# Turning the normalised attention outputs on VectorE instead of through DRAM by DMA

## The chip, the core and the metric

The kernel runs on one core of a Trainium2 chip. The core has TensorE (PE, matrix products into PSUM), VectorE (DVE), ScalarE (ACT), GpSimd (POOL) and SyncE (SP, which here only issues DMAs). They run side by side and wait for each other through semaphores. The metric is the device time of one execution in microseconds, lower is better; the time before is the median of three runs.

## The reference

Two pairs of layers work on x of 2048 rows by 512 columns, in bf16: a spectral filter, then an attention with 32 query heads of 16 columns and a single key and value head.

```python
x = x + _A_ref(_layernorm(x, axis=-1), A_w_r, A_w_i)      # A: irfft2(rfft2(x) * W)
x = x + _B_ref(_layernorm(x, axis=-1), B_wq, B_wk, B_wv, B_wo)
x = x + _A_ref(_layernorm(x, axis=-1), A_w_r, A_w_i)
x = x + _B_ref(_layernorm(x, axis=-1), B_wq, B_wk, B_wv, B_wo)
...
scores = jnp.einsum("bhqd,bkd->bhqk", q, k) * (Dh ** -0.5)   # in _B_ref
p = _softmax(scores, axis=-1)
o = jnp.einsum("bhqk,bkd->bhqd", p, v)
return (lambda x, *d: x.transpose(*d))(o, 0, 2, 1, 3).reshape(B, S, H * Dh) @ wo
```

## The kernel before, in words

**Stages.** Each pair is one `Layer`. Its front normalises rows, transposes them and runs the first Fourier matmuls; its middle and back (`add_middle`, `add_back`) finish the filter and make keys, values and the first query tiles; then its attention (`Attn`) runs. Fronts of the second layer for finished rows run inside the first layer's attention.

**Attention.** It is cut into 32 blocks: four query blocks of 512 rows (`qb`), four groups of eight heads (`g`), and two halves of a group (`par`), four heads each. A block has 16 key blocks of 128 and so 64 score tiles ("units") of 128 keys by 512 queries. The scores of four heads run side by side in four 32-row strips of TensorE. The exponential of a unit is taken in one of two ways. ScalarE takes an exact exp over two units at a time from a double PSUM bank `sa` (`exp`, L1346). VectorE takes an approximation from a single bank: one `tensor_scalar` makes a 16-bit integer whose bits are a bf16 number (`p1`, L1353), and two more phases, integer additions mostly on GpSimd (`phase`, L1357, or on VectorE, L1359), refine it. So an exact unit costs TensorE one value matmul (`pv`, L1363) and an approximated one three. Each value matmul also sums the weights, in a 17th column.

**Closing a block.** When the values of a block are summed, VectorE transposes the accumulator in 32x32 blocks into `raw` (`evac`, L1370). After the second half of a pair it takes reciprocals of the sums (`recip`, L1375) and multiplies (`mul`, L1381) into `on`, bf16, 128x512, with two buffers. `on` has queries in its partitions, and the output projection needs head columns there: it must be turned once more in blocks. In this kernel fifteen of the sixteen pairs of a layer go through DRAM: `norm_dma` issues four DMAs that write 32 partitions each into `onw` (L1401) and one transposing DMA that reads it back into `OT` (L1402), all from SP's queue. The last pair of a layer is turned by VectorE (`norm`, L1390).

**After four pairs of a query block.** `close_rows` adds the output projection (`proj`, L1406: four row tiles of four matmuls), the addition to x on VectorE (`close_x`, L1276; at the end of the first layer the addition is a fifth matmul instead, with statistics L1050 read from PSUM), and in the first layer the front of the next layer. For the last query block the projection of the first three groups is one task and that of the fourth another.

**What sets the order.** There is no loop order by hand. A planner (`Plan`) walks through modelled time, keeps modelled clocks of the four engines, and emits each engine's instructions in the order that comes out; on the chip the engines follow this order and semaphores. Units are dealt to ScalarE or VectorE by `deadline`: whoever would run dry first gets the next scores. All other work is a `Task` with an engine, a modelled duration, dependencies, a priority and perhaps a `lazy` time during which it only takes free moments. A `Mark` is an event without an instruction. For the turn by DMA the planner sets a mark at the end of the multiplication plus `OUT_TURN`, 25 us, before which nothing that reads the turned tile is placed. Query tiles of later groups (`add_qt`, L1325 on TensorE and L1285 for the copy) are tasks as well, asked for three blocks ahead. Where TensorE would be idle too long, `fill` emits matmuls on zeros (`dummy`, L1032 and L1036).

Of the kernel before, what the change touches and what calls it, by code (L numbers as in the profile page):

```python
# [10 lines left out]
P = 128  # L11
BF = mybir.dt.bfloat16
# [102 lines left out]
class Plan:  # L115
# [30 lines left out]
    PATIENT = 1000.0  # L146
    URGE = 150.0
    TURN = 7000.0
    OUT_TURN = 25000.0
    EARLY_SD = 0  # L150
    STARVED = 12000.0

# [442 lines left out]
class Attn:  # L595
# [74 lines left out]
    def done(self, b, slot, end):  # L670
        p, em = self.plan, self.em
        qb, g, par = self.blocks[b]
        self.left.discard(b)
        m = Mark("PE", end, slot)
        ev = p.add("DVE", 630.0, [m], lambda k: em.evac(self, b, slot), give=(m,), prio=-3)
        self.evac[b] = self.evac_last = ev
        if par == 0:
            return
        tail = 0.0 if b >= len(self.blocks) - 2 else 5000.0
        rc = p.add("DVE", 260.0, [ev, self.evac[b - 1]], lambda k: em.recip(self, b), lazy=tail)  # L680
        mu = p.add("DVE", 600.0, [rc], lambda k: em.mul(self, b), lazy=tail, port=True)
        if b < len(self.blocks) - 2:
            no = Mark("DMA", None)

            def turned(k):
                em.norm_dma(self, b)
                no.end = k.end + p.OUT_TURN

            mu.then = turned
        else:  # L690
            no = p.add("DVE", 626.0, [mu], lambda k: em.norm(self, b), lazy=tail)
        self.evac[b] = no
        if g == 3:
            self.layer.close_rows(qb, [self.evac[8 * qb + 2 * i + 1] for i in range(4)])
# [252 lines left out]
class Emit:  # L947
# [441 lines left out]
            at.OT[qb] = self.t4([4, 512])  # L1389
        self.nc.vector.transpose(out=at.OT[qb][:, g, :], in_=on.rearrange("p a h d -> p (a h d)"))  # L1390

    def norm_dma(self, at, b):

        qb, g, par = at.blocks[b]
        on = at.raw.pop((qb, g))
        if g == 0:
            at.OT[qb] = self.t4([4, 512])
        way = self.way.tile([512, P], BF, name="onw", tag="onw")
        rows = way.rearrange("(a q) (h c) -> h q a c", q=32, c=32)
        for h in range(4):  # L1400
            self.nc.sync.dma_start(out=rows[h], in_=on[32 * h:32 * h + 32].rearrange("p a h d -> p a (h d)"))  # L1401
        self.nc.sync.dma_start_transpose(out=at.OT[qb][:, g:g + 1, :], in_=way)  # L1402

    def proj(self, at, t, r, slot, g0, g1):
        for g in range(g0, min(g1, 4)):
            self.nc.tensor.matmul(self.ps(slot), lhsT=at.OT[t][:, g, r * P:(r + 1) * P], rhs=self.WO[:, g, :],  # L1406
                                  start=(g == 0), stop=(g == g1 - 1), skip_group_check=True)
# [89 lines left out]
```

## Time and profile before

| what | us |
|---|---|
| median of 3 runs | 1332.8 (1332.57 to 1332.93) |
| the profiled execution: its time, and its span | 1332.57, 1330.8 |
| first layer, attention: first to last approximated tile starts | 111.4 to 671.1 |
| second layer, attention: the same | 768.9 to 1318.3 |
| the 120 copies to DRAM: issue to landing, median | 1.9 |
| the 30 transposing DMAs, on their queue | 1.12 to 1.24 each |

In the profile, times count from the start of the span. "Busy" counts from the start of an operation to its end, and since the end of one overlaps the start of the next, starts of neighbours on a full engine stand closer together than the operations last. L numbers are lines of the kernel before. A line of the view in order of time has start, duration, engine, source line, operation, output and inputs with shapes, and in brackets the idle time before it and what ended it.

### The profile page before, as it was taken

To read this page: it belongs to the slowest core of one execution; us is meant where nothing else is said; L and a number is where in the kernel's file an instruction comes from. 1 tells how busy PE (TensorE), PEld (TensorE's weight loads), DVE (VectorE), ACT (ScalarE), POOL (GpSimd) and SP (SyncE) were. 2 spreads that over 40 slices of the span, in tenths; PEclk is the share of its full clock that TensorE was granted. 3 is DMA by queue.
4 is the path that set the end of the run, shared out by engine and by line. 5 is a ranking of instruction groups with operands and counts; after the bars stand their busy time and mean duration, and the time that the engine had idled before them with its cause. 6 is when DMAs were issued, how large, how long until landed. Compare 5 with 4: busy or idle time off the path is not lost. (4 is left out here: it accounts for less than half of the span.)

```text
span 1330.8 us, 31765 instructions
## 1 busy us (share of the span) xinstructions
PE 1291.0 (97%) x12968; PEld 438.2 (33%) x13032; DVE 1273.3 (96%) x2280; ACT 1226.4 (92%) x1396; POOL 842.0 (63%) x826
## 2 busy tenths in 40 slices
PE   9999999999999999999999999999999999999998
PEld 4643222222222223332256422223222322322232
DVE  6998999999999999999979999999999999999998
ACT  6478999999999999999954899999999999999996
POOL 0004787857777667766720067887677867786785
PEclk9999999999999999999999999999999999999999
DMA  9100000010000100010051000000100010000001
GB/s 294 41 1 1 10 9 10 10 41 10 5 7 12 39 9 10 9 41 10 9 166 41 1 1 9 10 10 9 25 10 10 10 25 6 9 14 22 5 9 25
DMA packets 108722, 33.05 MB, mean 25 GB/s; under 512 B 88352, under 2 KB 107296, under 8 KB 108576
## 3 DMA queue, kind: packets, MB, share of 16 engines
q1 hardware_dynamic: 108288, 30.46, 10.0%
q8 instruction: 102, 1.67, 0.5%
q10 hardware_dynamic: 288, 0.56, 0.1%
q14 instruction: 44, 0.36, 0.1%
HBM read 17.89 MB, written 7.60 MB: 19 GB/s over the span
## 5 line engine op out<-in xcount | busy, mean ns | idle before, releaser
L1341 PEld LDWEIGHTS <-KA 32*128 32x128 bf16 x2048 | 87.6, 91 | 234.1 <-issue 222.9
L1341 PEld LDWEIGHTS <-KB 32*128 32x128 bf16 x2048 | 85.2, 91 | 229.7 <-issue 224.1
L1363 PEld LDWEIGHTS <-vs_116 128*32 128x32 bf16 x2474 | 98.3, 94 | 97.2 <-issue 90.8
L1363 PEld LDWEIGHTS <-vs_117 128*32 128x32 bf16 x1622 | 97.7, 94 | 62.8 <-issue 60.6
L1363 PEld LDWEIGHTS <-vs_118 128*32 128x32 bf16 x1622 | 71.0, 93 | 75.6 <-issue 72.8
L1363 PEld LDWEIGHTS <-vs_119 128*32 128x32 bf16 x1622 | 72.0, 94 | 65.5 <-issue 57.5
L1357 POOL INT64_ADD w_1388<-w_1387 x1 | 1.0, 1039 | 110.5 <-DVE w_1387 L1353 110.5
L1357 POOL INT64_ADD w_11001<-w_11000 x1 | 1.0, 1037 | 98.3 <-PE b_69 L1341 98.3
L1050 DVE BATCH_NORM_STATS2 st<-x_sb 128x6 f32<-128x512 bf16 x52 | 35.4, 681 | 4.1 <-DMA x_sb<-in_A_x_dram 3.6
L1346 ACT ACTIVATE e_8_92<-sa_65 128x1024 bf16<-128x1024 f32 x32 | 35.5, 1110 | 2.4 <-PE sa_64 L1341 1.6
L1346 ACT ACTIVATE e_6_90<-sa_64 128x1024 bf16<-128x1024 f32 x33 | 36.5, 1106 | 0.0
L1346 ACT ACTIVATE e_13_97<-sa_65 128x1024 bf16<-128x1024 f32 x31 | 34.7, 1118 | 1.6 <-PE sa_64 L1341 1.6
L1346 ACT ACTIVATE e_1_85<-sa_64 128x1024 bf16<-128x1024 f32 x32 | 35.4, 1107 | 0.0
L1346 ACT ACTIVATE e_5_89<-sa_65 128x1024 bf16<-128x1024 f32 x30 | 33.5, 1118 | 1.6 <-PE sa_64 L1341 1.6
L1346 ACT ACTIVATE e_12_96<-sa_65 128x1024 bf16<-128x1024 f32 x31 | 34.1, 1100 | 0.9 <-PE b_69 L1341 0.8
L1346 ACT ACTIVATE e_19_103<-sa_65 128x1024 bf16<-128x1024 f32 x31 | 34.7, 1121 | 0.1
L1346 ACT ACTIVATE e_10_94<-sa_65 128x1024 bf16<-128x1024 f32 x30 | 33.2, 1106 | 1.7 <-PE sa_64 L1341 1.6
L1346 ACT ACTIVATE e_18_102<-sa_64 128x1024 bf16<-128x1024 f32 x31 | 34.6, 1115 | 0.1
L1346 ACT ACTIVATE e_2_86<-sa_65 128x1024 bf16<-128x1024 f32 x30 | 33.5, 1116 | 1.3 <-PE sa_64 L1341 1.0
L1346 ACT ACTIVATE e_9_93<-sa_64 128x1024 bf16<-128x1024 f32 x31 | 34.6, 1115 | 0.1
L1346 ACT ACTIVATE e_7_91<-sa_65 128x1024 bf16<-128x1024 f32 x31 | 34.4, 1110 | 0.1
L1346 ACT ACTIVATE e_15_99<-sa_64 128x1024 bf16<-128x1024 f32 x31 | 34.3, 1107 | 0.1
(4100 smaller groups left out, 6438.4 us busy)
## 6 DMA issues: line engine op xcount, KB each, us to landing
it<-const_IT SPq DMA_DIRECT2D x8, 640.0 KB, 6.1
onw<-on SPq DMA_DIRECT2D x120, 32.0 KB, 1.9
x_sb<-in_A_x_dram SPq DMA_DIRECT2D x4, 512.0 KB, 6.8
out_dram<-x_sb SPq DMA_DIRECT2D x16, 128.0 KB, 1.9
way<-x_sb SPq DMA_DIRECT2D x6, 256.0 KB, 2.4
tab_PH<-const_PH ACTq DMA_DIRECT2D x1, 512.0 KB, 4.9
w_131<-const_FT SPq DMA_DIRECT2D x1, 512.0 KB, 8.8
w_136<-const_FT SPq DMA_DIRECT2D x1, 512.0 KB, 8.4
```

The lines of the kernel that those rows point to most:

```text
L1050: self.nc.vector.bn_stats(st, self.ps(slot) if slot else self.x[:, x[1], x[0], :])
L1341: self.nc.tensor.matmul(o, lhsT=KX[rs, kc * P:(kc + 1) * P], rhs=at.QT[qb][rs, g, :], start=True, stop=True, skip_group_check=True)
L1346: self.wrote("ACT", e, self.nc.scalar.activation(out=e, in_=self.ps(slot), func=ACT.Exp, scale=SCALE))
L1357: self.nc.gpsimd.int64_add(t[p][:, 0:n].bitcast(U64), t[0][:, 0:n].bitcast(U64), DELTA[p] * FOUR)
L1363: self.nc.tensor.matmul(self.ps(slot)[32 * h:32 * h + 32, :], lhsT=V[:, kc, :], rhs=rhs, start=first, stop=last, skip_group_check=True)
```

## The change

All outputs are turned on VectorE by `norm`, as the last pair of each layer already was. The branch that called `norm_dma`, the function itself and the constant `OUT_TURN` go. The turn is now a task with a modelled 626 ns and the same `lazy` time as the multiplication (5 us, and none for the last pair); the tasks that read the turned tile wait for its end instead of for the mark 25 us after the multiplication.

```diff
-    OUT_TURN = 25000.0
...
         mu = p.add("DVE", 600.0, [rc], lambda k: em.mul(self, b), lazy=tail, port=True)
-        if b < len(self.blocks) - 2:
-            no = Mark("DMA", None)
-
-            def turned(k):
-                em.norm_dma(self, b)
-                no.end = k.end + p.OUT_TURN
-
-            mu.then = turned
-        else:
-            no = p.add("DVE", 626.0, [mu], lambda k: em.norm(self, b), lazy=tail)
+        no = p.add("DVE", 626.0, [mu], lambda k: em.norm(self, b), lazy=tail)
         self.evac[b] = no
...
-    def norm_dma(self, at, b):
-
-        qb, g, par = at.blocks[b]
-        on = at.raw.pop((qb, g))
-        if g == 0:
-            at.OT[qb] = self.t4([4, 512])
-        way = self.way.tile([512, P], BF, name="onw", tag="onw")
-        rows = way.rearrange("(a q) (h c) -> h q a c", q=32, c=32)
-        for h in range(4):
-            self.nc.sync.dma_start(out=rows[h], in_=on[32 * h:32 * h + 32].rearrange("p a h d -> p a (h d)"))
-        self.nc.sync.dma_start_transpose(out=at.OT[qb][:, g:g + 1, :], in_=way)
```

Since the planner deals all work anew, the change of one task's engine moves the order on every engine from the first closed pair on.

## The prediction

> **What bounds the kernel now.** I read the busy totals first, then the forty slices, then the busy time of each engine in stretches, and last the order of time on VectorE and ScalarE where a stretch was not full.
>
> ```profile
> span 1330.8 us, 31765 instructions
> PE 1291.0 (97%) x12968; PEld 438.2 (33%) x13032; DVE 1273.3 (96%) x2280; ACT 1226.4 (92%) x1396; POOL 842.0 (63%) x826
> ...
> DVE  6998999999999999999979999999999999999998
> ACT  6478999999999999999954899999999999999996
> ```
>
> The totals name three engines as candidates. The slices say where: VectorE and ScalarE are both full in the two attention stages (about 111 to 672 and 769 to 1319 us) and are short of work only in the spectral stages before each. TensorE's 97% is made of modelled ends, so I ask who waits for whom instead. The stretches (columns: PE, PEld, DVE, ACT, POOL busy, granted clock, DMA share, GB/s) give a steady piece of attention, one with a hole, and a spectral one:
>
> ```profile
> 166.00:200.00 34.00, 33.39 (x372) 9.58 (x360) 33.97 (x58) 33.95 (x39) 27.80 (x27) 1.00 0.06 9
> ...
> 266.00:299.00 33.00, 31.76 (x297) 9.49 (x293) 30.71 (x55) 31.40 (x37) 19.31 (x19) 1.00 0.20 42
> ...
> 699.00:732.00 33.00, 31.09 (x233) 20.70 (x236) 31.95 (x76) 14.45 (x27) 0.00 (x0) 1.00 0.14 41
> ```
>
> In the steady piece VectorE works 33.97 of 34 us and ScalarE 33.95, at a full clock: **two engines share one supply of score tiles and both are full**. A microsecond put on either lengthens the stage, unless units move to the other. In order of time VectorE shows its prices:
>
> ```profile
> 186.41 0.69 DVE L1353 TENSOR_SCALAR w_2543<-b_66 128x512 uint16<-128x512 f32 x1
> 187.02 0.71 DVE L1370 STREAM_TRANSPOSE raw<-b_69 128x512 f32<-128x512 f32 x1
> 187.65 0.65 DVE L1353 TENSOR_SCALAR w_2543<-b_67 128x512 uint16<-128x512 f32 x1
> ```
>
> On a full engine the price is the distance between starts, not the duration: 0.63 us for a 128x512 transpose that lasts 0.71. In the same way an approximated score tile (L1353) costs 0.60 us (median of 1622 distances), and an exp over two tiles (L1346) 0.905, though it lasts 1.10.
>
> The normalised output, by its tiles:
>
> ```profile
> L1401 SPq DMA_DIRECT2D onw<-on x120: 315/489/1557, 145.2 to 1300.7; - x120
> L1381 DVE TENSOR_TENSOR on<-raw,rc x32: 676/682/694, 144.5 to 1322.7; 128x512 bf16<-128x512 f32 x32
> L1390 DVE STREAM_TRANSPOSE w_8479<-on x1: 711/711/711, 676.3 to 676.3; 128x512 bf16<-128x512 bf16 x1
> L1390 DVE STREAM_TRANSPOSE w_17903<-on x1: 712/712/712, 1323.5 to 1323.5; 128x512 bf16<-128x512 bf16 x1
> ```
>
> Two of 32 outputs are turned on VectorE (711 ns each); thirty leave by four DMAs each and come back by a transposing DMA. Among the waits of VectorE and TensorE inside attention none is for one of those landings, so the DMA way costs them nothing that shows.
>
> **The change part by part.** *Added to VectorE:* 30 turns, 15 in each layer. The row of 711 ns is the operation itself, and the transpose from PSUM, of the same size and duration, costs 0.63 in a full stream: 30 x 0.63 = 18.9 us. The built order puts 2 to 10 places between the multiplication and its turn, so none waits for its input.
>
> A rule against this price: the Trainium skill, "VectorE: DVE Perf Modes", section "The three transpose paths", gives 311 ns for one 128x128 in bf16 on VectorE. Four of those would be an estimate of 1.24 us for our tile, 37.3 us for thirty, 18.4 us more than the sum here; the rows of 711 ns contradict it, so it is not used.
>
> *Removed:* 120 DMAs and 30 transposing DMAs on SP's queue, and VectorE's wait for the buffer that those DMAs read. Nothing behind them gets faster that anyone waits for: the other loads and turns of that queue show no waiting reader in attention. I price this at 0. It is bounded by SP's own waits for the copies, 2.5 us at most, and 0.
>
> *Moved: score units.* The kernel's planner hands tiles to whichever engine would run dry first, so work put on VectorE sends units to ScalarE. The built program shows how many. Approximated tiles go from 805 to 800 in the first layer and from 817 to 810 in the second; exps from 622 to 624 and from 616 to 619. VectorE's work between its first and last score tile then grows by 15 x 0.63 - 5 x 0.60 = 6.4 us and 15 x 0.63 - 7 x 0.60 = 5.3 us, together 11.7. ScalarE's grows by 2 x 0.905 = 1.8 and 3 x 0.905 = 2.7, together 4.5. TensorE loses 24 value matmuls (six groups of four at 0.22 us, 1.3 us) and 28 strip fillers, GpSimd 7 additions; neither is full (27.80 of 34 us for GpSimd), so I count them as nothing, and if that cover went the 1.3 us would be a gain.
>
> Both sums can't be right at once. If VectorE stays as full as now, the time grows by 11.7 and ScalarE idles 7.2 us more; if ScalarE does, it grows by 4.5 and VectorE must find 7.2 us in its present holes. Those holes are few. From first to last score tile VectorE has 546.9 us of work (each operation's count by its distance) in 560.3, and 538.1 in 550.0: 13.4 and 11.9 us of holes, most of it in these stalls and their like, where TensorE is late with the next query tile:
>
> ```profile
> DVE w_14548 L1285 <- PE b_68 L1325: 1.9, 1, 1.9
> DVE w_2777 L1285 <- PE b_69 L1325: 1.9, 1, 1.9
> DVE w_12390 L1285 <- PE b_69 L1325: 1.9, 1, 1.9
> DVE w_16706 L1285 <- PE b_67 L1325: 1.9, 1, 1.9
> ```
>
> These happen where two query projections stand back to back on TensorE's queue (eight full matmuls with no scores between). In the built programs I find four such pairs inside attention in both kernels, so I leave the stalls as they are. In full stretches VectorE idles less (0.1 to 0.3 us in 20) than ScalarE (0.3 to 0.7), so it is the tighter one and I go two thirds of the way to its sum: 4.5 + 2/3 x 7.2 = 9.3 us.
>
> *Freed: the output projections.* The planner held each DMA-turned output back for 25 us before it would place the projection. At the ends of the layers this has put all sixteen projections behind the last turn, row by row:
>
> ```profile
> 1323.46 0.71 DVE L1390 STREAM_TRANSPOSE w_17903<-on 128x512 bf16<-128x512 bf16 x1
> 1324.66 0.69 DVE L1276 TENSOR_TENSOR x_sb<-b_68,x_sb 128x512 bf16<-128x512 f32 x1 [0.48 <-PE b_68 L1406]
> 1325.52 0.69 DVE L1276 TENSOR_TENSOR x_sb<-b_66,x_sb 128x512 bf16<-128x512 f32 x1 [0.17 <-PE b_66 L1406]
> 1326.39 0.69 DVE L1276 TENSOR_TENSOR x_sb<-b_67,x_sb 128x512 bf16<-128x512 f32 x1 [0.17 <-PE b_67 L1406]
> 1327.25 0.69 DVE L1276 TENSOR_TENSOR x_sb<-b_69,x_sb 128x512 bf16<-128x512 f32 x1 [0.17 <-PE b_69 L1406]
> ```
>
> The closing additions stand 0.86 us apart (four matmuls at 0.216) where VectorE needs 0.60. In the changed program nine projections stand ahead of the last ones, so rows two and three follow at 0.60. The fourth addition would start at 1324.66 + 3 x 0.60 = 1326.46 instead of 1327.25: 0.8 us less. At the end of the first layer only two rows come early (bank order), and by the same reckoning the statistics, now 1.08 apart, would end 1.1 us sooner; but the middle matmuls that TensorE does meanwhile move behind. Between 0 and 1.1 I take 0.6. Together 1.4 saved, between 0.8 and 1.9.
>
> **Sum.** The profiled execution took 1332.57 us (span 1330.8 and 1.8 around it). 1332.57 + 9.3 - 1.4 = 1340.5. The median of the three runs is 0.2 above the profiled one: **1340.7 us**. Ends: 4.5 - 1.9 = +2.6 and 11.7 - 0.8 = +10.9, so 1335.4 and 1343.7.
>
> **The rivals.** *ScalarE sets the pace.* VectorE fills its holes with turns, which may wait (the planner lets a turn idle up to 5 us for a free moment). For it: a turn needs nothing from TensorE, and at 604 us VectorE stands still 1.6 us while ScalarE works on. Against it: most holes are stalls that both engines share. Time: +2.6, 1335.4 us.
>
> *Faster: the late query tiles go away.* The 25 us hold crowds the projections of a finished query block right behind the two query projections (eight full matmuls, and sixteen from 273.9 us on); released early, TensorE's load spreads and the stalls need not occur. ScalarE shows each at 1.6 us (waiting until 272.53), so four give 6.3: 4.5 - 1.4 - 6.3 = -3.2, 1329.6 us. It decides only if all four go and ScalarE's sum binds: with three, the rest is within what can be told from no change (0.2%, 2.7 us). Against: the changed order still has four back-to-back pairs.
>
> *Slower: the turns collide with GpSimd.* Where VectorE and GpSimd overlapped at 1319.6 us, a one-tile addition (L1359) lasted 1.12 us instead of 0.58: 0.54 lost. The two turns of the trace ran while GpSimd stood still, so they don't say whether a turn can be held that way. GpSimd is busy 0.8 of the time; a loss of half of 0.54 on thirty turns is 8.1 us, on VectorE's sum: 11.7 + 8.1 - 1.4 = +18.4, 1351.2 us. Against: the PSUM transposes cost 0.63 beside a busy GpSimd, and the bf16 turn takes as long as the f32 one (711 and 708 ns), so it runs at the same plain pace.
>
> The Trainium skill, "SBUF — State Buffer", section "Who interferes with whom", says that a VectorE instruction with a single SBUF input and outside the two-port modes doesn't contend with GpSimd. By it this rival costs nothing; no run here shows that yet.
>
> **How the numbers follow.** The shared-load case 0.70, ScalarE's pace 0.17, late tiles gone 0.06, collision 0.07. Within 0.2% fall half of the second case, the low edge of the first and a sixth of the third: 0.12. Faster: 0.05. Slower: 0.83. The range leaves out the third and fourth cases and reaches a little under the low end of the second and over +10.9: 1334.5 to 1345.0. The likeliest case alone is 1336 to 1344.
>
> **What would show it.** Right: 32 turns of about 0.71 us on VectorE, the next operation 0.63 after them; both engines as full as now; first-layer attention 4 to 6 us longer; more idle on ScalarE than on VectorE; closing additions 0.60 apart. Turns longer than 0.8 us would mean the collision, fewer waits of L1285 for query projections the faster rival. The forecast would be most wrong if the reshuffled order made or removed several stalls of 2 us, which I can count only as pairs on a queue.

## The result, and the profile after

The changed kernel is slower: 1340.81 us (median of four, 1340.6 to 1341.0) against 1332.68 for the kernel before beside it, a ratio of 1.0061 with a 95% interval of 1.0043 to 1.0078. The profiled execution took 1340.67 us with a span of 1338.9, so the span grew by 8.1 us.

The busy totals and the slices of the kernel after:

```profile
span 1338.9 us, 31412 instructions
...
PE 1298.0 (97%) x12913; PEld 438.9 (33%) x12982; DVE 1281.7 (96%) x2297; ACT 1231.0 (92%) x1401; POOL 834.9 (62%) x819
...
DVE  6998999999999999999979999999999999999998
ACT  6478999999999999999944899999999999999996
```

VectorE is busy 8.4 us longer, about as much as the span grew, and ScalarE 4.6 us longer. The slices have the same shape: nothing new stands still for long. The same steady stretch as before (columns: PE, PEld, VectorE, ScalarE and GpSimd busy, granted clock, DMA share, GB/s):

```profile
166.00:200.00 34.00, 33.19 (x358) 9.80 (x352) 33.70 (x57) 33.94 (x39) 25.79 (x25) 1.00 0.01 1
```

ScalarE is as full as it was, VectorE 0.3 us less so. The clock is full, and the DMA share is down from 0.06 to 0.01.

Where the 8.1 us are is read by stages, each attention from the start of its first approximated tile to that of its last: 110.8 to 671.1 and 768.9 to 1318.3 us before, 110.9 to 675.7 and 773.1 to 1327.7 after. (The table of times before has 111.4 for the first of these, the start of the second tile; the first starts at 110.81.)

| us | before | after | change | predicted |
|---|---|---|---|---|
| attention, first layer | 560.3 | 564.8 | +4.5 | |
| attention, second layer | 549.4 | 554.6 | +5.2 | |
| both | 1109.7 | 1119.4 | +9.7 | +9.3 |
| last tile of layer one to first of layer two | 97.8 | 97.4 | -0.4 | -0.6 |
| last tile to the end | 12.5 | 11.2 | -1.3 | -0.8 |

The two stretches of the kernel before, then those of the kernel after (columns as above):

```profile
110.80:671.10 560.30, 548.62 (x5728) 162.21 (x5754) 551.07 (x939) 557.27 (x615) 415.35 (x406) 1.00 0.09 16
768.90:1318.30 549.40, 538.03 (x5705) 161.09 (x5719) 540.08 (x904) 543.97 (x591) 420.18 (x406) 1.00 0.07 12
...
110.90:675.70 564.80, 552.95 (x5719) 165.04 (x5741) 555.44 (x950) 560.69 (x618) 412.27 (x404) 1.00 0.04 10
773.10:1327.70 554.60, 543.53 (x5697) 160.79 (x5717) 544.85 (x911) 547.86 (x595) 417.18 (x403) 1.00 0.01 4
```

Added up, ScalarE is busy 1108.6 us of 1119.4 after and 1101.2 of 1109.7 before. Its work grew by 7.3 us and its idle time by 2.4, from 8.5 to 10.9. VectorE went from 1091.2 to 1100.3, 9.1 us more work, and from 18.6 to 19.1 us idle. So of the 9.7 us most is work, on both engines. The prediction had 11.7 for VectorE and 4.5 for ScalarE, but counted another way: each operation by its usual distance to the next. Counted so on the two traces, VectorE's work grew by 11.6 us and ScalarE's by 6.4.

The turns, by the tiles they read, and the first of them in the order of time on VectorE:

```profile
L1380 DVE STREAM_TRANSPOSE w_1974<-on x4: 701/702/703, 150.1 to 257.8; 128x512 bf16<-128x512 bf16 x4
...
L1380 DVE STREAM_TRANSPOSE w_17924<-on x4: 693/702/711, 1244.2 to 1332.5; 128x512 bf16<-128x512 bf16 x4
```

```profile
149.55 0.68 DVE L1343 TENSOR_SCALAR w_1932<-b_66 128x512 uint16<-128x512 f32 x1
150.15 0.70 DVE L1380 STREAM_TRANSPOSE w_1974<-on 128x512 bf16<-128x512 bf16 x1
150.77 0.65 DVE L1343 TENSOR_SCALAR w_1985<-b_67 128x512 uint16<-128x512 f32 x1
```

A turn lasts 0.70 us and the next operation starts 0.62 us after it. GpSimd ran an addition from 150.40 us on, beside the last 0.45 us of that turn (order of time on GpSimd):

```profile
148.90 1.04 POOL L1347 INT64_ADD w_1901<-w_1899  x1
150.40 1.04 POOL L1347 INT64_ADD w_1933<-w_1932  x1 [0.46 <-DVE w_1932 L1343]
```

The turn lasts no longer than the others and the addition no longer than the one before it. In the whole trace 28 of the 32 turns ran beside an addition; every turn took 0.69 to 0.71 us, and the additions beside them 1.03 to 1.04 us. So the collision is out. VectorE's waits for query tiles, one line each, and the long waits of ScalarE inside attention, in its order of time:

```profile
DVE w_2549 L1275 <- PE b_68 L1315: 2.0, 1, 2.0
DVE w_14123 L1275 <- PE b_66 L1315: 1.6, 1, 1.6
...
DVE w_12048 L1275 <- PE b_66 L1315: 1.0, 1, 1.0
```

```profile
460.50 1.02 ACT L1336 ACTIVATE e_18_102<-sa_65 128x1024 bf16<-128x1024 f32 x1 [2.56 <-PE sa_64 L1331]
...
1293.16 1.02 ACT L1336 ACTIVATE e_17_101<-sa_65 128x1024 bf16<-128x1024 f32 x1 [2.22 <-PE sa_64 L1331]
```

Before, VectorE waited four times about 1.9 us for a query tile and once 1.2; now it waits 2.0, 1.6, 1.0 and 0.4. ScalarE's waits of 1 us and more changed from four of 1.57 us (6.3) to four of 1.4 to 2.6 us (7.5 together). VectorE got 4.0 us back there, and ScalarE lost 1.2.

Lastly the end of the kernel on VectorE, from the last turn on, and the place between the layers that answers to it:

```profile
1332.52 0.71 DVE L1380 STREAM_TRANSPOSE w_17924<-on 128x512 bf16<-128x512 bf16 x1
1333.72 0.69 DVE L1266 TENSOR_TENSOR x_sb<-b_69,x_sb 128x512 bf16<-128x512 f32 x1 [0.48 <-PE b_69 L1384]
1334.33 0.68 DVE L1266 TENSOR_TENSOR x_sb<-b_67,x_sb 128x512 bf16<-128x512 f32 x1
1334.92 0.68 DVE L1266 TENSOR_TENSOR x_sb<-b_68,x_sb 128x512 bf16<-128x512 f32 x1
1335.52 0.68 DVE L1266 TENSOR_TENSOR x_sb<-b_66,x_sb 128x512 bf16<-128x512 f32 x1
```

```profile
680.64 0.71 DVE L1380 STREAM_TRANSPOSE w_8371<-on 128x512 bf16<-128x512 bf16 x1
...
682.33 0.70 DVE L1040 BATCH_NORM_STATS2 st<-b_69 128x6 f32<-128x512 f32 x1 [0.98 <-PE b_69 L1259]
...
684.17 0.70 DVE L1040 BATCH_NORM_STATS2 st<-b_67 128x6 f32<-128x512 f32 x1 [0.92 <-ACT x_sb L1262]
```

The closing additions now stand 0.60 us apart. Between the layers the second row's statistics come no sooner: ScalarE's copy of the row is in front of them.

### The profile page after: what moved, and what is told of

It is laid out like the page before. It is cut to its first block, busy times and chain, and to the rows that moved or that the text cites. A ratio compares the mean times of both kernels' runs of the same rounds, so it can differ in the third digit from the quotient of the medians.

```text
span 1338.9 us, 31412 instructions
## 1 busy us (share of the span) xinstructions
PE 1298.0 (97%) x12913; PEld 438.9 (33%) x12982; DVE 1281.7 (96%) x2297; ACT 1231.0 (92%) x1401; POOL 834.9 (62%) x819
## 4 chain that ended last, share of the span: by engine, by line
ACT 48%; PE 30%; DVE 17%; issue 2%; DMA 1%; SPq 1%; POOL 0%; DVEq 0%; POOLq 0%
PE sa_64 L1331 3%; PE b_66 L1353 3%; PE b_69 L1353 3%; PE b_67 L1353 3%; ACT e_5_89 L1336 2%; ACT e_3_87 L1336 2%; ACT e_4_88 L1336 2%; ACT e_16_100 L1336 2%; PE sa_65 L1331 2%; ACT e_10_94 L1336 2%; ACT e_11_95 L1336 2%; ACT e_15_99 L1336 2%; ACT e_8_92 L1336 2%; ACT e_14_98 L1336 2%; ACT e_9_93 L1336 2%; ACT e_20_104 L1336 2%
## 5 line engine op out<-in xcount | busy, mean ns | idle before, releaser
L1331 PEld LDWEIGHTS <-KB 32*128 32x128 bf16 x2048 | 89.0, 91 | 229.0 <-issue 221.5
L1331 PEld LDWEIGHTS <-KA 32*128 32x128 bf16 x2048 | 83.4, 91 | 229.0 <-issue 219.4
L1353 PEld LDWEIGHTS <-vs_116 128*32 128x32 bf16 x2486 | 102.1, 94 | 97.6 <-issue 91.4
L1353 PEld LDWEIGHTS <-vs_117 128*32 128x32 bf16 x1610 | 97.1, 94 | 69.8 <-issue 68.1
L1353 PEld LDWEIGHTS <-vs_118 128*32 128x32 bf16 x1610 | 73.1, 94 | 75.7 <-issue 70.8
L1353 PEld LDWEIGHTS <-vs_119 128*32 128x32 bf16 x1610 | 71.9, 94 | 72.5 <-issue 67.9
```

Source lines behind the costliest of these rows:

```text
L1331: self.nc.tensor.matmul(o, lhsT=KX[rs, kc * P:(kc + 1) * P], rhs=at.QT[qb][rs, g, :], start=True, stop=True, skip_group_check=True)
L1353: self.nc.tensor.matmul(self.ps(slot)[32 * h:32 * h + 32, :], lhsT=V[:, kc, :], rhs=rhs, start=first, stop=last, skip_group_check=True)
```

## The experiments

The theory: thirty turns at 0.63 us are shared by two full engines, because the planner gives score units to ScalarE in return. Its rivals: VectorE alone or ScalarE alone sets the pace, or the reshuffled order does. Every ratio is against the kernel before, measured beside it. Kernels 1, 2, 6, 7 and 8 change only what is named, while VectorE, ScalarE and TensorE keep the order of all their other instructions; in the others the planner makes its order anew. Stages and waits are read from each kernel's one profiled execution.

**1. The turns alone, in the order of before.**

```diff
             def turned(k):
-                em.norm_dma(self, b)
+                em.norm(self, b)
                 no.end = k.end + p.OUT_TURN
```

> Order and planned split of the kernel before, unchanged; only the thirty turns are done by VectorE, each directly behind its multiplication, in place of the DMAs. Output as the reference. Shared load (mine): with the units nailed down, ScalarE can take nothing over, so nearly the whole of 30 x 0.63 = 18.9 us, and up to 0.1 us each for waiting on the multiplication, lands on the end: 1351 us, between 1347 and 1355. Rival, the reshuffled order is what made the changed kernel slower and a turn of 0.63 us finds room in VectorE's 25 us of holes: under 1336 us.

1348.96 us (1347.95 to 1350.13), ratio 1.0121 (1.0107 to 1.0135): 16.0 us longer, of 18.9 that thirty turns cost by their distance. The steady stretch:

```profile
166.00:200.00 34.00, 33.29 (x364) 9.35 (x360) 33.97 (x58) 33.55 (x38) 27.16 (x27) 1.00 0.01 1
```

Where no unit may move, VectorE is full, ScalarE idles 0.4 us more, and nearly the whole work is on the path: attention grew by 15.5 us. The price of a turn holds. In the changed kernel, where the planner moves units to ScalarE, attention grew by 9.7, so the sharing is worth 5.8.

**2. The order of after, with the turns taken off VectorE.** Twenty-four of the thirty turns that the change moved go through DRAM again, at their places in the changed order (`norm_dma` is put back for it).

```diff
-        no = p.add("DVE", 626.0, [mu], lambda k: em.norm(self, b), lazy=tail)
+        way = em.norm_dma if g < 3 and b < len(self.blocks) - 2 else em.norm
+        no = p.add("DVE", 626.0, [mu], lambda k: way(self, b), lazy=tail)
```

> Order and planned split of the changed kernel, but 24 of its 30 turns (all but those of the fourth head group) go by DMA, so 24 x 0.63 = 15.1 us of VectorE's work vanish at a fixed order. Output as the reference. Shared load (mine): ScalarE has as many exps as in the changed kernel and is nearly full there, so only part of it comes back, 2 to 8 us: 1337 us. Rival, VectorE alone sets the pace: all 15.1 come back, 1326 us. Rival, the order is the cause and not the work: 1340 to 1341 us.

1340.99 us (1340.7 to 1344.24), ratio 1.0066 (1.0053 to 1.008): nothing came back, a miss for the theory as I had put it. VectorE's holes (a stretch less its work in it, counts by distances, as in the prediction) went from 11.5 and 11.3 us in the changed kernel to 18.9 and 18.7, together 14.8 us more, and 24 x 0.63 = 15.1: all that was taken off turned into idle time. The steady stretch, and VectorE's largest wait over both layers (for scores of its approximated tiles: total, times, longest):

```profile
166.00:200.00 34.00, 33.46 (x356) 9.69 (x349) 33.20 (x57) 33.94 (x38) 25.61 (x25) 1.00 0.06 9
```

```profile
DVE w L1344 <- PE b L1332: 11.0, 31, 1.0
```

TensorE's own largest wait there is for ScalarE, whose exp has to empty a double bank before the next scores:

```profile
PE sa L1332 <- ACT e L1337: 8.8, 39, 0.5
```

VectorE is down to 33.20 of 34 us and waits for scores; ScalarE stays at 33.94. The DMAs put back are not what holds it: of TensorE's and VectorE's waits in attention one alone, of 0.12 us, is for a landing. So in the changed order VectorE's work alone doesn't set the time: that rival is out.

**3. The turn on VectorE, its readers held back 25 us as before.**

```diff
+    OUT_TURN = 25000.0
...
-        no = p.add("DVE", 626.0, [mu], lambda k: em.norm(self, b), lazy=tail)
+        no = nm = p.add("DVE", 626.0, [mu], lambda k: em.norm(self, b), lazy=tail)
+        if b < len(self.blocks) - 2:
+            no = Mark("DMA", None)
+
+            def turned(k):
+                no.end = k.end + p.OUT_TURN
+
+            nm.then = turned
```

> The changed kernel with the planner's hold of 25 us put back, now counted from the end of VectorE's turn. Approximated tiles 792 and 812, exps 628 and 618: VectorE's work is 1.6 and 6.4 us above that of the kernel before, ScalarE's 5.4 and 1.8. Shared load: by my two-thirds rule 7.2 + 2/3 x 0.8 = 7.7 us, with nothing freed at the ends of the layers: 1340.4 us, so about the changed kernel's time, its gain at the ends lost and its load a little better dealt. The closing additions stand 0.86 us apart again. Rival, the early release is what costs (it reshuffles the order): back at 1333 to 1335 us.

1355.3 us (1354.42 to 1357.26), ratio 1.017 (1.0156 to 1.0184), 15 us over what I expected. The profiled execution is the slowest of the four, 1357.26. In it attention is 2.3 us longer than in the changed kernel (567.1 and 554.5 us), with two dips of the granted clock to 0.73 and 0.77 over 5 us. The rest, 13.9 us, is at the layer ends: 103.0 us between the layers instead of 97.4, and 19.5 at the end instead of 11.2. VectorE's waits say for what (total, times, longest), and TensorE's order of time at the end what stands there instead:

```profile
DVE x_sb L1274 <- PE b L1392: 11.2, 8, 7.9
...
DVE st L1048 <- PE b L1267: 8.4, 4, 7.9
```

```profile
1338.82 9.68 PE L1034 MATMUL b<-zero 128*32 128x512 bf16 x176
1348.43 3.63 PE L1392 MATMUL b<-WO,w 128*128 128x512 bf16 x16
```

The last pair with a hold is turned less than 25 us before the layer ends (at 1323.8 us in the second layer). So its projection is placed behind everything else, 9.7 us of matmuls on zeros among it, and additions and statistics stand 7.9 us for it. Whether the hold costs anything in the middle of attention, experiment 11 tells.

**4. The DMA way with a short hold.**

```diff
-    OUT_TURN = 25000.0
+    OUT_TURN = 7000.0
```

> The kernel before with a hold of 7 us instead of 25. The planner then gives VectorE 5 approximated tiles more in each layer (810 and 822) and ScalarE 3 exps fewer: VectorE's work +3.0 and +3.0 us, ScalarE's -2.7 and -2.7. Shared load by the two-thirds rule: -5.4 + 2/3 x 11.4 = +2.2, less 1.7 freed at the ends of the layers as in the changed kernel: 1333.2 us. If ScalarE set the pace: 1325.6; if VectorE alone: 1337.0. Rival, the hold alone matters: 1331 us or below.

1335.93 us (1335.52 to 1337.68, ten runs), ratio 1.0025 (1.0015 to 1.0034). Early release in both layers costs 3 us without a turn on VectorE: attention grew by 3.4 and 0.8 us, and ScalarE waits 1 us or more six times, 15.6 us in all, instead of four times, 6.3. I had expected it to be the same as before within half a microsecond; reshuffling is not free in either direction.

**5. The short hold for the last DMA pair of each layer alone.**

```diff
-                no.end = k.end + p.OUT_TURN
+                no.end = k.end + (p.OUT_TURN if b < len(self.blocks) - 4 else 7000.0)
```

> The kernel before with the hold cut from 25 to 7 us for the last DMA-turned pair of each layer alone. Tiles and exps dealt as in the kernel before (805 and 817, 622 and 616), and the order of the first layer's attention is untouched. If the freed projections are worth what I said, the ends shrink by 0.8 at the output and by 0.6 (0 to 1.1) between the layers, as far as the second layer's reshuffled order brings nothing of its own: 1331.4 us. If they are worth nothing: 1332.9.

1331.78 us (1331.47 to 1332.0, eleven runs) beside 1332.69 (28 runs, 1332.38 to 1333.04), ratio 0.9993 (0.9985 to 1.0002). Every run lies below every run of before, 0.9 us at the median, though the interval of the ratio touches 1. This is the freed projection by itself. VectorE's order of time at the end:

```profile
1323.17 0.71 DVE L1390 STREAM_TRANSPOSE w<-on 128x512 bf16<-128x512 bf16 x1
1324.37 2.48 DVE L1276 TENSOR_TENSOR x_sb<-b,x_sb 128x512 bf16<-128x512 f32 x4 [0.49 <-PE b L1406]
```

Four additions in one run of 2.48 us, 0.60 apart: the last tile to the end takes 11.7 us instead of 12.5, the 0.8 us that the prediction had worked out for the output. Between the layers, where 0.6 was expected, 0.1 came (97.7 us). Of all kernels here this is the fastest.

**6 and 7. Shorter exps in the order of after, with the turns on VectorE and without.** Each exp writes 504 of 512 columns of a tile. The eight columns left out hold what the buffer held last, approximated tiles and spectral differences among it: GpSimd writes ones into them once at the start (21 small operations, not shown), but the buffers are used for other tiles in between, so the expectations' remark that they hold ones is not so. Kernel 7 adds the edit of 2.

```diff
-out=e, in_=self.ps(slot), func=ACT.Exp
+out=e[:, :, 0:504], in_=self.ps(slot)[:, :, 0:504], func=ACT.Exp
```

> The changed kernel in its order, but each exp leaves out the last 8 of the 512 columns of a tile (they hold ones): about 13 ns of 905, over 1243 exps some 16 us of ScalarE's work less. Two engines that both set the pace: nothing comes back alone, 1339 to 1341 us, as nothing came back when 15 us were taken from VectorE alone. ScalarE alone sets the pace at this order: 1325 to 1328.

> The same order, with both taken away: 24 of 30 turns by DMA (15.1 us of VectorE's work) and each exp 8 columns short per tile (some 16 us of ScalarE's). Two engines that both set the pace: now most of it comes back, 10 to 15 us, 1326 to 1331. If TensorE's queue, or its order, is what sets the pace: nothing comes back here either, 1339 to 1341.

Kernel 6: 1335.44 us (1333.73 to 1337.76), ratio 1.0023 (1.0013 to 1.0034). Kernel 7: 1332.98 us (1332.26 to 1337.55), ratio 1.001 (1.0001 to 1.0019). Both scatter more than the others, because the granted clock dipped in part of the executions; the fastest ones, two of seven and five of ten, at a mean clock of 0.999 to 1.0, took 1333.7 to 1333.9 and 1332.3 to 1332.5. The groups by line, all exps in one line (busy time, mean ns | idle time ahead of them and its releasers), in kernels 2, 6 and 7:

```profile
L1337 ACT ACTIVATE e<-sa 128x1024 bf16<-128x1024 f32 x1243 | 1148.7, 1129 | 15.1 <-PE sa L1332 11.5 <-PE b L1332 2.6
```

```profile
L1338 ACT ACTIVATE e<-sa 128x1008 bf16<-128x1008 f32 x1243 | 1138.5, 1048 | 18.7 <-PE sa L1333 11.8 <-PE b L1333 4.5
```

```profile
L1339 ACT ACTIVATE e<-sa 128x1008 bf16<-128x1008 f32 x1243 | 1138.4, 1057 | 20.1 <-PE sa L1334 11.6 <-PE b L1334 6.1
```

The dose is read from the distance between starts, as every price here: the median from one exp to the next is 0.904 us in kernel 2 and 0.890 in 6 and 7, so it is 14 ns on 1243 exps, 17 us, about as set down. (Busy time fell by 10.3 us only; it counts each exp to its end wherever the next one comes later.) So of 17 us off ScalarE 5.4 come back, 7.0 in the fastest executions; of 15 off VectorE none (2); and with both off 7.8 to 8.4. Both cases set down for kernel 6 missed: nothing, or nearly all. In the changed order **ScalarE is the tighter engine**, but it doesn't set the time alone. VectorE stands close behind it: its turns are worth nothing until ScalarE has been relieved, and then 1.4 to 2.5 us. That is the reverse of what I had taken. The rest of ScalarE's gain became later starts: the time by which exps start further apart than the median grew from 29.5 us in kernel 2 to 40.2 in kernel 6. Part of it is plain waiting for scores from TensorE, 18.7 and 20.1 us of idle time instead of 15.1 (the profiled executions of both kernels have a dip in them).

**8. Twice the DMAs.** In the order of before every DMA turn is done a second time, into a tile that nothing reads.

```diff
         self.nc.sync.dma_start_transpose(out=at.OT[qb][:, g:g + 1, :], in_=way)
+        way = self.way.tile([512, P], BF, name="onx", tag="onx")
...
+        again = self.pool.tile([P, 1, 512], BF, name="again", tag="again", bufs=2)
+        self.nc.sync.dma_start_transpose(out=again, in_=way)
```

> The kernel before with each turn by DMA done twice, the second time into a tile that nobody reads: 150 DMAs more on SP's queue and 7.9 MB more each way at the most, order and units as before. I priced the removal of one set at 0, so doubling it should cost 0: 1332.9, within 0.7 us. If the DMAs cost something that the waits don't show: above 1334.

1337.82 us (1334.38 to 1339.34), ratio 1.0035 (1.0025 to 1.0046), where I had expected no change. Nearly the whole of it comes from the first layer's attention (4.5 us longer in the profiled execution), from one place near 590 us. SP's queue in order of time, and TensorE there:

```profile
583.70 2.17 SPq L1406 DMA_DIRECT2D onx<-on  x4
...
587.35 1.12 SPq L1408 DMA_TRANSPOSE again<-onx  x1
...
588.52 0.58 SPq L1092 DMA_DIRECT2D way<-x_sb  x1
590.99 1.26 SPq L1085 DMA_TRANSPOSE e<-way  x1
```

```profile
593.11 0.39 PE L1341 MATMUL b<-w,KB 32*128 32x512 bf16 x1
595.86 0.71 PE L1121 MATMUL b<-tab_PH,e 128*128 128x512 bf16 x2 [2.37 <-DMA e<-way]
596.51 0.60 PE L1341 MATMUL b<-w,KB 32*128 32x512 bf16 x1
```

The row turn of x for the next layer's front (L1092, L1085) uses the same queue and stands behind the second copy and its turn. Its transposing DMA is issued at 590.99 us and lands at 595.8; in before it was issued at 585.80 and landed at 588.9, 4.2 us ahead of the matmul that reads it. TensorE now waits 2.37 us for it. The executions without a dip of the clock took 1334.4 and 1335.0, 1.7 to 2.3 more than before: about this one wait. The other doubled turns cost nothing that shows, and before has no such wait. So the DMAs of before cost nothing that their removal could give back, as the prediction had it.

**9. Half the dose.** Odd groups are turned by VectorE, even ones by DMA with the hold of 25 us.

```diff
-        if b < len(self.blocks) - 2:
+        if b < len(self.blocks) - 2 and g % 2 == 0:
```

> Every second pair (odd head groups) is turned by VectorE, the others by DMA with the hold of 25 us: half the dose. Tiles 804 and 810, exps 622 and 619: VectorE's work +4.0 us in all, ScalarE's +2.7. Shared load by the two-thirds rule: +3.6 us, nothing freed at the ends, 1336.3 us. Rival, the order makes the time and not the load: no reason for a value halfway, so 1333 or 1340 are as likely.

1340.82 us (1340.4 to 1340.97), ratio 1.006 (1.0045 to 1.0075): as slow as the full change. But the stages differ: attention grew by 3.8 us, which is the dose's share as expected (3.6), and the ends by 1.5 and 2.6. At the end of the kernel, VectorE:

```profile
1328.74 0.71 DVE L1390 STREAM_TRANSPOSE w<-on 128x512 bf16<-128x512 bf16 x1
...
1333.03 0.69 DVE L1276 TENSOR_TENSOR x_sb<-b,x_sb 128x512 bf16<-128x512 f32 x1 [3.58 <-PE b L1406]
```

3.58 us of waiting for projections that the last held pair kept back, the stall of 3 in small.

**10. Twice the dose.** Every turn that the change moved is done twice, and modelled as 1252 ns.

```diff
-        no = p.add("DVE", 626.0, [mu], lambda k: em.norm(self, b), lazy=tail)
+        no = p.add("DVE", 626.0 if b >= len(self.blocks) - 2 else 1252.0, [mu], ...
...
+        if b < len(at.blocks) - 2:
+            again = self.pool.tile([P, 512], BF, name="again", tag="again", bufs=2)
+            self.nc.vector.transpose(out=again, in_=on.rearrange("p a h d -> p (a h d)"))
```

> Each of the thirty turns is done twice by VectorE, the second time into a tile that nobody reads, and the planner knows it (1252 ns): double dose. Tiles 790 and 800, exps 629 and 624: VectorE's work +18.6 us, ScalarE's +13.5. Shared load: 16.9 - 1.7 = +15.2, 1347.9 us, of 37.8 us added. VectorE alone: +37.8 would show as 1369. Order and not load: near 1341.

1343.28 us (1343.18 to 1343.59), ratio 1.0079 (1.0063 to 1.0096). Attention grew by 12.4 us where the two-thirds rule gave 16.9 and ScalarE's sum alone 13.5. In the two stretches VectorE is busy 16.8 us more than before and idle 4.5 less, ScalarE busy 14.8 more and idle 2.4 less: this order wastes less, why is not shown.

**11. The hold without its reach past the end.** As 3, but with `b < len(self.blocks) - 4`.

> As the changed kernel with the hold of 25 us put back, but not for the last two pairs of a layer. If the excess of that earlier run (1355.3 against 1340.4 expected) came from the two stalls of 7.9 us at the ends of the layers, where the held-back projections came too late, it is gone here: VectorE's work +8.0, ScalarE's +7.2, 7.7 - 1.7 = +6.0, 1338.7 us. If the hold itself costs inside attention: 1350 or more.

1340.42 us (1340.25 to 1341.96), ratio 1.006 (1.0045 to 1.0075): the time of the changed kernel, with 97.5 and 11.3 us at the ends, 13.7 us less than in experiment 3. So the 15 us of experiment 3 were nearly all the two stalls, and with the turn on VectorE the hold inside attention is worth nothing measurable.

**12. Another order with the same work.** The planner is told 640 ns instead of 626 for a turn; the instructions are those of the change, a few units dealt otherwise.

```diff
-        no = p.add("DVE", 626.0, [mu], lambda k: em.norm(self, b), lazy=tail)
+        no = p.add("DVE", 640.0, [mu], lambda k: em.norm(self, b), lazy=tail)
```

> The changed kernel with a turn modelled at 640 ns instead of 626, which makes no difference on the chip but deals the work anew. Tiles 798 and 810, exps 625 and 619: VectorE's work +10.4, ScalarE's +5.4, 8.7 - 1.7 = +7.0, 1339.7 us. It measures how much the order alone scatters: I expect within 2 us of the changed kernel. If order is the cause, it could as well return to 1333.

1337.64 us (1337.49 to 1337.69), ratio 1.0036 (1.0023 to 1.0049): 3.2 us faster than the change as made, where I had expected a difference of 2 at most, with attention at 565.6 and 550.7 us. The first layer is 0.8 us longer than in the changed kernel and the second 3.9 shorter. A change of 14 ns in a model is worth more than a third of what was to be explained, and still the kernel is slower than before. The profile says where the difference lies: ScalarE is busy 0.4 us more than in the changed kernel and idle 3.4 us less (7.4 instead of 10.9), and its waits of 1 us and more are three, 4.2 us in all, instead of four, 7.5. Its waits for scores in this order (total, times, longest):

```profile
ACT e L1336 <- PE sa L1331: 6.3, 10, 1.6
```

In the changed kernel the same waits add up to 9.7 us. So the 3 us between two orders of nearly the same work are ScalarE's long waits for scores.

Attention against dose, by the same stages (both layers, less before's 1109.7). The rule is the prediction's two thirds of the way from ScalarE's sum to VectorE's, worked out for each built order:

| turns on VectorE | growth, us | by the rule | ScalarE's busy time | ScalarE's idle time |
|---|---|---|---|---|
| none, short hold (4) | 4.2 | 2.2 | -4.9 | +9.1 |
| half (9) | 3.8 | 3.6 | +3.6 | +0.2 |
| all, modelled 640 (12) | 6.7 | 8.7 | +7.7 | -1.0 |
| all, held in the middle (11) | 8.9 | 7.7 | +8.7 | +0.2 |
| all, the change | 9.7 | 9.3 | +7.3 | +2.4 |
| all, twice (10) | 12.4 | 16.9 | +14.8 | -2.4 |

From half to all to twice the growth rises with the work added, and each order strays from the rule by 0.2 to 2.0 us up to the full dose and 4.5 us at twice. The last two columns add up to the growth by their definition, but they part it in two. Where turns were added, most of the growth is work that the planner gave to ScalarE, and an order's luck is ScalarE's idle time, up to 2.4 us either way. Where none were added (4), ScalarE had less work, and its idle time makes up more than the whole of the growth.

## Why the prediction was right, and where its reasons were not

*The price of a turn* (18.9 us for thirty): right. 32 turns of 0.69 to 0.71 us, the next operation 0.61 to 0.63 after 30 of them (behind the last turn of each layer it waits), and 16.0 us on the path where nothing else may move (experiment 1). The estimate of 1.24 us from the Trainium skill, "VectorE: DVE Perf Modes", section "The three transpose paths", is now contradicted by 32 rows instead of two.

*DMAs cost nothing*: right for before. Doubling them costs only where a queue neighbour has a waiting reader (8). One caution belongs to it: at that one place the row turn of before lands only 4.2 us ahead of its reader.

*The collision with GpSimd*: refuted by the rows at 150.15 us and the 27 other turns that ran beside an addition. The Trainium skill, "SBUF — State Buffer", section "Who interferes with whom", says that an operation of VectorE with one SBUF input outside the two-port modes doesn't contend with GpSimd; the trace now agrees, with 0.70 us beside a running GpSimd.

*The shared load* (+9.3, measured +9.7): right as a mechanism, wrong in the reason for its size and in one of its two sums. Unshared the turns cost 15.5 us in attention (1), shared 9.7, so the time does lie between the two sums. The step that failed is "In full stretches VectorE idles less [...], so it is the tighter one and I go two thirds of the way to its sum". In the order after, VectorE's turns gave nothing back (2), and ScalarE's shortened exps 5.4 to 7.0 of 17 us (6). Small idle times of the order before told nothing of that. They didn't even agree among themselves: in full stretches, by distances, VectorE idled less, but by busy time over the two stretches ScalarE did, 8.5 us against 18.6.

The term that was mis-sized is ScalarE's sum of 4.5 us. Within the two stretches ScalarE runs seven more instructions (618 and 595 instead of 615 and 591), and seven more exps, 1193 instead of 1186: 7 x 0.905 = 6.3 us. The step had counted exps over whole layers, where only five are added, so two of them lay outside the stretches before. By busy time its work grew by 7.3; the remaining 1.0 us is not taken apart. ScalarE idles 2.4 us more, where the rule implied 9.3 - 4.5 = 4.8. VectorE's sum was right: 11.7 reckoned, 11.6 when the trace is counted the same way. (From start to start the second stretch of before is 549.4 us and not 550.0, so its holes were 11.3 us and not 11.9.) The rival that named ScalarE's pace was nearer on the engine, but its sum was 1.8 us too small and it allowed ScalarE no more idle time. That two thirds landed 0.4 us from the stage is partly luck, for two orders of nearly the same work differ by about 3 us (12).

*"Four such pairs in both kernels, so I leave the stalls as they are"*: wrong in the count and harmless in the sum. The built order has three pairs of query projections directly next to each other; the fourth is separated. VectorE's waits for query tiles shrank from 9.0 to 5.0 us, but on ScalarE, the tighter engine, the long waits grew by 1.2. The faster rival needed all four gone there.

*The freed projections* (-1.4 us): measured -1.7 at the ends, but only about 0.8 of it is the freed projections. At the output -1.3 (-0.8 predicted): from the last turn to the fourth addition it is 3.00 us instead of 3.79, as worked out, and the last turn follows the last approximated tile after 4.80 us instead of 5.17, which the step had not looked at. Between the layers -0.4 (-0.6): the statistics gained nothing, the last of the four starts 5.16 us after the last turn where it was 5.17, since the second row's wait 0.92 us for ScalarE's copy of the row, a reader that the step hadn't looked at either. About half of the 0.4 is again the way from the last tile to the last turn. Experiment 5 agrees: 0.9 us for the freed projections alone, nearly all at the output. So the predicted 0.6 between the layers failed, and that the term came out near is luck.

So the sum is right to 0.1 us and its two terms to 0.4, but the larger term stands on a sum that was 1.8 us too small and a share whose reason was wrong, about half of the smaller came from elsewhere, and an order of nearly the same work moves the whole by 3.

What stays open: why one order has longer waits of ScalarE for scores than another of nearly the same work (the waits account for the 3 us of experiment 12), and what limits the changed order once both engines have room (TensorE's queue, with scores, values and projections in one order, is the candidate; no run here relieves it alone). With some 32 us taken off the two engines together, about 8 came back, so this limit is near.

## What to carry to other kernels

Where two engines share a supply of work and both are full, price added work by the distance between starts, work out both engines' sums in the built program with every instruction that moves, and expect a time between unshared and evenly shared; which of the two is tighter can't be read from small idle times of the old order, because the order changes with the work. A planner's hold or deadline is checked at the ends of the stages, where it can reach past the last work: one hold cost some 14 us there and nothing measurable in the middle. And a total that agrees to 0.1 us proves no split: try a second order of the same work before trusting a difference of 3 us. The same rule of distances holds for an experiment's dose: by busy time the shortened exps seemed worth 10 us, by distances 17.

## What the runs showed of the hardware that I had not expected

After TensorE's wait of 2.37 us in experiment 8 the granted clock fell (windows of that kernel, columns as above):

```profile
590.00:595.00 5.00, 3.49 (x49) 0.98 (x46) 4.54 (x9) 4.63 (x7) 3.20 (x4) 1.00 0.68 93
595.00:600.00 5.00, 4.14 (x18) 0.77 (x18) 2.24 (x4) 2.75 (x4) 1.51 (x2) 0.62 0.38 98
600.00:605.00 5.00, 5.00 (x51) 1.23 (x47) 3.78 (x7) 3.29 (x4) 3.19 (x4) 0.69 0.00 0
605.00:610.00 5.00, 4.96 (x40) 1.44 (x37) 3.39 (x6) 5.00 (x7) 3.83 (x4) 1.00 0.00 0
```

Read in windows of 1 us, the clock is 0.50 from 597 to 603 us. A score matmul lasted 0.60 us instead of 0.39, and in the window from 600 us on the engines it feeds were down to about two thirds to three quarters of full work (3.78 and 3.29 of 5 us). The executions with a dip were about 3 us longer than those without, so the dip cost more than the wait; two of the eight kept a mean clock of 1.0. So the wait is not shown to be the cause, and dips came without one too: in kernels 3, 6 and 7 no wait of TensorE over 0.2 us stands in the 15 us ahead of them. In kernel 7:

```profile
1110.00:1120.00 10.00, 9.36 (x66) 1.80 (x65) 7.94 (x14) 7.62 (x9) 4.39 (x5) 0.65 0.00 0
```

The traces' record of the granted clock holds it at a half for 3.4 us in kernel 6 and twice 3.4 in the attention of kernel 3, 6.8 in kernel 8 and 10.2 in kernel 7. What sets these dips off is open. The Trainium skill, "TensorE: Matmul & The Clock Gate", section "What's actually happening", has the clock fall after at least one idle window of about 3.4 us; here a wait of 2.37 us stood ahead of one fall and none over 0.2 us ahead of the others, and the measurement decides. Before, whose longest wait of TensorE between 111 and 1325 us is 1.7, kept a mean clock of 0.999 or 1.0 in all 28 executions beside these.
